# Attention with a sink and a window, then a feed-forward layer: more products of ones between TensorE's first visits

## The chip, the cores and the metric

The kernel runs on one core of a Trainium2 chip. The metric is the time of one execution in microseconds on the device, the median of several runs.

## What is computed

Queries, keys and values have 4 batches, 8 heads, 768 positions and 64 columns. Each position sees the 128 positions up to itself and the first 4 (the sink). The heads are joined to a table of 3072 rows by 512, which goes through two matrices with an ELU between them.

```python
keep = is_sink | in_window
scores = np.where(keep, scale * q @ k.T, -1e9)
a = np.exp(scores - scores.max(-1))
x = (a / (a.sum(-1) + 1e-9)) @ v
h = x @ w_in
g = np.where(h > 0.0, h, np.exp(np.minimum(h, 0.0)) - 1.0)
out = g @ w_out
```

## The kernel before, in words

The 3072 rows are cut into tiles of 128 and the tiles into ten chunks of two or three. For each chunk the attention of four pairs of heads makes the table x, and a feed-forward part runs x through the two matrices in 16 steps: the product with `w_in` (L900, writes the PSUM bank h), ELU, and the product with `w_out` (L930, adds up in acc). Attention of the next chunk is put between the steps of the feed-forward part.

The work is written as tasks, each for one engine with an estimated duration and with the tasks that it depends on (`plan.add`). `Plan.order` tries a few hundred orders with those estimates and keeps the best; `keep_order` then emits all tasks in that order and ties each engine's instructions to one another, so that every engine works through a fixed list. A task of TensorE (PE in the rows) is called a visit here. TensorE does its list strictly in that order.

The first chunk has nothing to hide behind. Its attention is `attention_f32`: for each step the scores of two heads (L599, into banks s or acc), a masked minimum on VectorE (DVE, L606), an exponential on ScalarE (ACT, L609), a transpose of the result on TensorE (L616, into one of the two banks h), a copy of that bank to the tile pt by DVE or ACT (L620), and the product with the values (L657, with L665 for the sums). The transposes write columns 0 to 255 of their bank.

TensorE also computes products that nobody reads: 128 by 128 ones times 128 by 248 ones in bf16, made by `warm`, in columns 264 to 511 of a bank. Nine stand ahead of all other work (L1278), one before the first visit (L1050). For the other visits that the plan's estimate starts before 28 us, L1052 counts how many fit between the end of the visit before and the start of this one, at 0.11 us each with 0.2 us kept free, and `filled` puts them right ahead of the visit. They go to the second bank h, or to the second bank s where the visit before starts after 7.0 us by the plan. The framework adds a semaphore wait wherever a tile that is still to be read would be written again; it follows whole tiles, here a bank.

```python
ones_k, ones_n = (nc.const_aps.tensor(1.0, [P, n], BF16) for n in (P, DM - 2 * KW))

def warm(to):
    nc.tensor.matmul(to[:, 2 * KW :], ones_k, ones_n, start=True, stop=True)
```

Of the kernel before, what the change touches and what calls it, by code (L numbers as in the profile page):

```python
# [44 lines left out]
HALF = NF // 2  # L45
PARTS = [(0, 0, HALF), (1, 0, HALF), (0, HALF, NF), (1, HALF, NF)] + [(c, 0, NF) for c in range(2, len(SIZES))]
LAG = 2
EARLY, WARM_UNTIL = 9, 28.0
NEAR = 1
WHOLE = 3  # L50
TURNED = 2
# [46 lines left out]
class Plan:  # L98
# [17 lines left out]
    def add(self, eng, dur, fn, *args, deps=(), lat=0.0, pos=None, or_=(), gap=2.0, port=None, mode=None):  # L116

        t = Task(eng, dur, fn, args, deps, lat, pos, gap, port, mode)
        for way in or_:
            t.ways[way[0]] = way[1:]  # L120
        self.tasks.append(t)
        return t
# [272 lines left out]
def fast_path(tc, ctx, first, kq, vx, wt, out, nw, inside, flag, limits):  # L395
# [9 lines left out]
    def banks(name, n):  # L405
        return rows(name, [P, 512], F32, n, psum)
# [22 lines left out]
    h_ps, s_ps, po_ps = banks("h", 2), banks("s", 2), [first["end"]]  # L429
# [572 lines left out]
    for c in range(WHOLE, len(SIZES)):  # L1002

        kts = key_tiles(CHUNKS[c])
        a = kts.index(CHUNKS[c][0])
        a = a * KW if all(any(g in ch for ch in CHUNKS[WHOLE:]) for g in kts[:a]) else 0
# [33 lines left out]
    a = add("DVE", 1.45, in_range, deps=[*seen, *exps_done[:-2], limits_])  # L1040
    a = add("DVE", 0.2, last_in_range, deps=[a, *exps_done[-2:]])
    b = add("PE", 0.1, lambda: nc.tensor.matmul(sp[:, 0:3], ones, some16, start=True, stop=True), deps=[a], pos=start - 3.0)
# [6 lines left out]
    pe = sorted((t for t in tasks if t.eng == "PE" and t.start < WARM_UNTIL), key=lambda t: t.start)  # L1049
    pe[0].fn = filled(pe[0].fn, first["warm"], h_ps[1], 1)  # L1050
    for a, b in zip(pe, pe[1:]):
        b.fn = filled(b.fn, first["warm"], s_ps[1] if a.start > 7.0 else h_ps[1], int((b.start - a.start - a.dur - 0.2) / 0.11))  # L1052
    keep_order(tc, tasks, first["spread"])


def filled(fn, warm, to, n):

    def run(*args):
        for _ in range(n):
            warm(to)  # L1060
        fn(*args)

    return run
# [5 lines left out]
def keep_order(tc, tasks, first):  # L1069

    bb = tc.nc.cur_bb.bb
    seen = len(bb.instructions)
    prev = {first.engine: first.name}
    base = tc.cur_priority
    for i, t in enumerate(tasks):
        tc.cur_priority = base + 10 * i
        t.fn(*t.args)
        new = bb.instructions[seen:]
        seen += len(new)
        for ins in new:  # L1080
            if ins.engine in prev:
                tc.add_manual_dep(ins, prev[ins.engine], mybir.DependencyInfo(mybir.DependencyClass.NoSync, mybir.DependencyReason.DATA), reason="order")
            prev[ins.engine] = ins.name
# [169 lines left out]
def attention_moe(tc, kq, vx, words_in, wt, out):  # L1253
    nc = tc.nc
    with ExitStack() as ctx:
# [51 lines left out]
        with ExitStack() as inner:  # L1307
            fast_path(tc, inner, first, kq, vx, wt, out, nw, f[:, 0:1], flag, limits)
# [38 lines left out]
```

## Time and profile before

| what | value |
|---|---|
| median of 3 runs | 616.5 us |
| lowest and highest | 615.62, 616.95 us |
| the profiled execution's own time | 616.32 us |
| its span, first to last instruction | 614.5 us |
| TensorE busy | 604.5 us, 98% |
| VectorE, ScalarE, GpSimd busy | 485.0, 450.3, 271.5 us |

The shares are means over the whole span. The change lies in its first 30 us, so the timeline of that stretch is what to read, engine by engine: start, duration, line, tiles and count, and in brackets the idle time ahead of a row with what ended it. Idle times that are shorter than 0.15 us are not shown. Rows of one kind that follow one another are merged, and a merged row of TensorE ends with the pipeline of its last product.

### The profile page before, as it was taken

How to read it: one execution, taken by the hardware profiler on the slowest of the kernel's cores; microseconds unless marked ns; L12 is line 12 of the kernel's file. 1: busy time of each engine (PE TensorE's matmuls, PEld its weight loads, DVE VectorE, ACT ScalarE, POOL GpSimd, SP SyncE). 2: the span in 40 equal slices, each digit the busy share in tenths (PEclk: the TensorE clock that was granted, in tenths of full speed). 3: DMA queues.
4: the chain of work that ended last, by engine and by line, in shares of the span. 5: the costliest groups of instructions: out<-in, count | busy, mean ns of one | idle time of the engine just before them, and what ended most of it. 6: DMA issues, size and time to landing. Idle time of an engine off the chain costs nothing.

```text
span 614.5 us, 14283 instructions
## 1 busy us (share of the span) xinstructions
PE 604.5 (98%) x4797; PEld 384.3 (63%) x4797; DVE 485.0 (79%) x1330; ACT 450.3 (73%) x1313; POOL 271.5 (44%) x545
## 2 busy tenths in 40 slices
PE   9998999999999999999999999999999999999996
PEld 6764666677665555676655556766555567665553
DVE  6998899899986657899997689999976899732232
ACT  5999999789876656888776678986766789642222
POOL 3787777345533233454333334443433435422211
PEclk9999999999999999999999999999999999999999
DMA  8688956879867256878772659898736596800001
GB/s 305 237 300 246 269 217 197 210 166 223 195 159 208 59 125 138 224 195 200 191 205 74 184 116 250 185 222 179 197 100 162 133 236 133 182 26 10 0 2 57
DMA packets 127428, 103.18 MB, mean 168 GB/s; under 512 B 96498, under 2 KB 102898, under 8 KB 127346
## 3 DMA queue, kind: packets, MB, share of 16 engines
q1 hardware_dynamic: 127200, 102.12, 64.3%
q8 instruction: 39, 0.64, 0.4%
q14 instruction: 43, 0.35, 0.2%
q10 hardware_dynamic: 146, 0.07, 0.0%
HBM read 71.75 MB, written 7.34 MB: 129 GB/s over the span
## 4 chain that ended last, share of the span: by engine, by line
PE 83%; ACT 10%; DVE 3%; issue 1%; DMA 1%; POOL 0%; DVEq 0%; ACTq 0%
PE h L900 35%; PE acc L930 29%; PE last_acc L930 6%; PE s L790 3%; PE s L791 3%; PE last_end L860 2%; PE s L860 2%; ACT w L501 2%; ACT last_acc L338 2%; ACT g L908 1%; ACT wu L341 1%; ACT gh L914 1%; ACT e L814 1%; DMA pt<-pq 1%; ACT e L609 1%
## 5 line engine op out<-in xcount | busy, mean ns | idle before, releaser
L900 PE MATMUL h<-x,w 128*128 128x256 f16 (+1 forms) x1920 | 275.7, 294 | 2.6 <-DVE gl L916 1.9
L900 PEld LDWEIGHTS <-w 128*128 128x128 f16 x1920 | 186.7, 98 | 78.2 <-issue 3.7
L919 POOL TENSOR_TENSOR gl<-g,gh 128x256 f16<-128x256 f32 (+1 forms) x143 | 119.9, 839 | 184.7 <-ACT gh L914 145.6
L930 PE MATMUL acc<-w,gh 128*128 128x512 f16 x636 | 175.0, 379 | 0.0
L930 PEld LDWEIGHTS <-gh 128*128 128x128 f16 x792 | 75.0, 98 | 66.7 <-issue 0.9
L908 ACT ACTIVATE g<-h 128x256 f32<-128x256 f32 (+1 forms) x160 | 66.8, 417 | 66.9 <-PE h L900 62.3
L914 ACT ACTIVATE gh<-g 128x256 f16<-128x256 f32 (+1 forms) x143 | 65.4, 458 | 48.7 <-DVE g L913 47.9
L930 PE MATMUL acc<-w,gl 128*128 128x512 f16 x318 | 96.9, 379 | 0.0
L814 ACT ACTIVATE e<-e,st 128x264 f32<-128x264 f32 x160 | 80.9, 506 | 17.0 <-DVE st L812 16.6
L910 DVE TENSOR_SCALAR g<-g 128x256 f32<-128x256 f32 (+1 forms) x99 | 35.5, 359 | 71.8 <-ACT g L908 70.9
L827 DVE SCALAR_TENSOR_TENSOR pq<-e,st,pq 128x256 f16<-128x256 f32 x160 | 86.0, 557 | 6.0 <-ACT pq L826 4.9
L826 ACT ACTIVATE pq<-e,st 128x256 f16<-128x256 f32 x160 | 75.1, 499 | 4.9 <-ACT g L908 2.0
L913 DVE SCALAR_TENSOR_TENSOR g<-g,h 128x256 f32<-128x256 f32 (+1 forms) x144 | 68.3, 474 | 4.8 <-ACT g L910 3.0
L812 DVE CUSTOM_DVE_ANT_0 e<-s,m 128x264 f32<-128x264 f32 x160 | 64.3, 425 | 9.2 <-PE s L791 8.3
L930 PEld LDWEIGHTS <-gl 128*128 128x128 f16 x396 | 38.1, 98 | 44.2
L716 ACT ACTIVATE kq<-kqs 128x912 f16<-128x912 f32 (+1 forms) x56 | 47.9, 860 | 6.9 <-PE s L791 5.1
L818 POOL TENSOR_SCALAR st<-st 128x2 f32<-128x2 f32 x80 | 19.3, 241 | 75.1 <-ACT e L814 66.8
L930 PE MATMUL last_acc<-w,gh 128*128 128x512 f16 (+1 forms) x126 | 45.3, 366 | 0.0
L502 POOL TENSOR_TENSOR w<-wv,w 128x512 f16<-128x512 f32 x32 | 38.0, 1192 | 9.0 <-ACT w L501 8.1
L719 DVE SCALAR_TENSOR_TENSOR kq<-kqs,kq 128x528 f16<-128x528 f32 (+1 forms) x56 | 38.1, 680 | 2.7 <-ACT kq L716 1.9
L790 PE MATMUL s<-kq 128*128 128x264 f16 x144 | 37.0, 276 | 0.6 <-ACT pq L826 0.6
L791 PE MATMUL s<-kq 128*128 128x264 f16 x144 | 36.9, 276 | 0.0
(155 smaller groups left out, 825.3 us busy)
## 6 DMA issues: line engine op xcount, KB each, us to landing
raw<-in_wt_dram SPq DMA_DIRECT2D x32, 512.0 KB, 5.7
kqs<-in_kq_dram SPq DMA_DIRECT2D x32, 456.0 KB, 3.8
kqs<-in_kq_dram SPq DMA_DIRECT2D x28, 326.0 KB, 3.5
out_dram<-wv SPq DMA_DIRECT2D x21, 256.0 KB, 4.5
vs<-in_vx_dram SPq DMA_DIRECT2D x16, 320.0 KB, 3.8
qk<-in_kq_dram SPq DMA_DIRECT2D x24, 195.0 KB, 4.5
vs<-in_vx_dram SPq DMA_DIRECT2D x16, 256.0 KB, 3.4
qk<-in_kq_dram SPq DMA_DIRECT2D x24, 163.0 KB, 4.1
```

What stands on the lines that cost most here:

```text
L790: nc.tensor.matmul(sp[:, :wd], q, hi[:, c0 : c0 + wd], start=True, stop=False)
L791: nc.tensor.matmul(sp[:, :wd], q, lo[:, c0 : c0 + wd], start=False, stop=True)
L812: red = add("DVE", 0.08 + 0.00104 * wd, lambda ee=ee, me=me, sp=sps[e], m=m, wd=wd: nc.vector.tensor_tensor_reduce(ee, sp[:, :wd], m[:, :w ...
L814: ex = add("ACT", act_us(wd, sums=True), lambda ee=ee, me=me, rs=rs[:, e : e + 1]: nc.scalar.activation(ee, ee, AF.Exp, bias=me, scale=-1. ...
L826: a = add("ACT", act_us(nb * P, True), lambda src=src, hi=hi, re=re: nc.scalar.activation(hi, src, AF.Copy, scale=re), deps=[rr])
L827: b = add("DVE", dve_us(nb * P) + 0.03, lambda src=src, hi=hi, lo=lo, re=re: nc.vector.scalar_tensor_tensor(lo, src, re, hi, ALU.mult, ALU ...
L900: nc.tensor.matmul(hp[:, :n], win[:, part, d, :], xx[:, :n], start=k == 0, stop=k == 3 * ND - 1)
L908: a = add("ACT", act_us(n) + 0.06, lambda gf=gf, hp=hp, sums=sums: nc.scalar.activation(gf, hp[:, :n], AF.Exp, scale=1.0 / G_SCALE, accum_ ...
L913: b = add("DVE", dve_us(n) - 0.035, lambda gf=gf, gd=gd, hp=hp: nc.vector.scalar_tensor_tensor(gd, gf, 0.0, hp[:, :n], ALU.min, ALU.max), ...
L914: th = add("ACT", act_us(n) - (0.03 if near else 0.0), lambda gd=gd, gh=gh: nc.scalar.activation(gh[:, :n], gd, AF.Copy), deps=[b])
L919: tl = add("POOL", pool_us(n), lambda gl=gl, gd=gd, gh=gh: nc.gpsimd.tensor_tensor(gl[:, :n], gd, gh[:, :n], ALU.subtract), deps=[th])
L930: nc.tensor.matmul(to[:, : cols.stop - cols.start], gg[:, i * P : (i + 1) * P], wout[:, part, cols], start=f == f0 and k == 0, stop=f == f ...
```

## The change

A second constant is added, and the count of products ahead of a visit changes in two ways: 0.1 us is kept free instead of 0.2, and visits that the plan starts before 8.5 us get one more.

```diff
-EARLY, WARM_UNTIL = 9, 28.0
+EARLY, WARM_BY, WARM_UNTIL = 9, 8.5, 28.0
...
     for a, b in zip(pe, pe[1:]):
-        b.fn = filled(b.fn, first["warm"], s_ps[1] if a.start > 7.0 else h_ps[1], int((b.start - a.start - a.dur - 0.2) / 0.11))
+        b.fn = filled(b.fn, first["warm"], s_ps[1] if a.start > 7.0 else h_ps[1], int((b.start - a.start - a.dur - 0.1) / 0.11 + (b.start < WARM_BY)))
```

Eleven products are added, and nothing else moves on any engine: four early (one ahead of the second scores, one between the two pairs of transposes, two ahead of the third scores) and seven later, one at each of seven visits.

TensorE's list before, from the first transposes to the third scores. `h0_184` and `h1_185` are the two banks h, `e0` to `e2` hold exponentials, `vm0_108` holds the queries and keys of the third step:

```order
L616 MATMUL h0_184<-ident_192,e0_109 128x128 [waits Activation_49,Pool_49]
L616 MATMUL h0_184<-ident_192,e0_109 128x128
L616 MATMUL h1_185<-ident_192,e1_110 128x128 [waits Activation_49]
L616 MATMUL h1_185<-ident_192,e1_110 128x128
L599 MATMUL s0_186<-vm0_108 128x132 [waits DMAHW4_49,DVE_49]
L599 MATMUL s1_187<-vm0_108 128x132 [waits DVE_49]
```

The same place with the change:

```order
L616 MATMUL h0_184<-ident_192,e0_109 128x128 [waits Activation_49,Pool_49]
L616 MATMUL h0_184<-ident_192,e0_109 128x128
L1276 LDWEIGHTS const-bfloat16-1.0
L1276 MATMUL h1_185<-const-bfloat16-1.0 128x248
L616 MATMUL h1_185<-ident_192,e1_110 128x128 [waits Activation_49]
L616 MATMUL h1_185<-ident_192,e1_110 128x128
L1276 LDWEIGHTS const-bfloat16-1.0
L1276 MATMUL h1_185<-const-bfloat16-1.0 128x248 [waits DVE_49]
L1276 LDWEIGHTS const-bfloat16-1.0
L1276 MATMUL h1_185<-const-bfloat16-1.0 128x248
L599 MATMUL s0_186<-vm0_108 128x132 [waits DMAHW4_49]
L599 MATMUL s1_187<-vm0_108 128x132
```

Three products of ones have come in, two of them behind the transposes into the same bank `h1_185`, the first of these with a wait for DVE; the scores behind them no longer carry one.

One of the later places on TensorE, around the transposes at 21.07 us and the scores at 21.44 us in the trace of before, as a difference (`s_187` is the second bank s):

```order
 L1276 MATMUL s_187<-const-bfloat16-1.0 128x248
+L1276 LDWEIGHTS const-bfloat16-1.0
+L1276 MATMUL s_187<-const-bfloat16-1.0 128x248
 L616 MATMUL last_end<-ident,e_111 128x128 x2
+L1276 LDWEIGHTS const-bfloat16-1.0
+L1276 MATMUL s_187<-const-bfloat16-1.0 128x248
 L599 MATMUL s_186<-kqs_82 128x132
 L599 MATMUL s_187<-kqs_82 128x132
```

A gap that had products has one more, and between the transposes and the scores, where there was none, one stands now.

## Rows read from the trace of the kernel before

**Rows 1.** The page: busy time by engine, and the granted clock.

```profile
PE 604.5 (98%) x4797; PEld 384.3 (63%) x4797; DVE 485.0 (79%) x1330; ACT 450.3 (73%) x1313; POOL 271.5 (44%) x545
...
PEclk9999999999999999999999999999999999999999
```

**Rows 2.** Timeline of PE, 0 to 13 us: start, us, line, tiles, count.

```profile
0.78 2.02 PE L1276 MATMUL last_acc<-const-bfloat16-1.0 128*128 128x248 bf16 x9 [0.78 <-PEq L1338]
...
5.30 0.81 PE L599 MATMUL s<-kqs 64*128 64x132 f32 x4 [0.41 <-DVE st L606]
...
6.48 1.11 PE L616 MATMUL h<-ident,e 128*128 128x128 f32 x4
7.52 0.81 PE L599 MATMUL s<-vm 64*128 64x132 f32 x4
8.27 0.69 PE L616 MATMUL h<-ident,e 128*128 128x128 f32 x2
...
11.41 0.81 PE L599 MATMUL acc<-vm 64*128 64x132 f32 x4
12.15 0.57 PE L616 MATMUL h<-ident,e 128*128 128x128 f32 x2
12.66 0.50 PE L599 MATMUL s<-vm 64*128 64x132 f32 x4
```

**Rows 3.** Line L1276, 0 to 3 and 14 to 30 us: duration ns min/median/max.

```profile
L1276 PE MATMUL last_acc<-const-bfloat16-1.0 x9: 366/411/412, 0.8 to 2.4; 128*128 128x248 bf16 x9
...
L1276 PE MATMUL s<-const-bfloat16-1.0 x32: 266/271/282, 14.8 to 29.1; 128*128 128x248 bf16 x32
```

**Rows 4.** Timeline of DVE, 7 to 9 us.

```profile
7.21 0.42 DVE L620 COPY pt<-h 128x256 f32<-128x256 f32 x1 [0.49 <-PE h L616]
...
7.63 0.42 DVE L620 COPY pt<-h 128x256 f32<-128x256 f32 x1
```

**Rows 5.** Timeline of PE, 14 to 30 us, at the products of ones.

```profile
14.81 0.81 PE L1276 MATMUL s<-const-bfloat16-1.0 128*128 128x248 bf16 x6
15.55 0.44 PE L657 MATMUL last_end<-pt,vm 128*64 128x128 f32 x4
...
19.95 1.15 PE L1276 MATMUL s<-const-bfloat16-1.0 128*128 128x248 bf16 x9
21.07 0.44 PE L616 MATMUL last_end<-ident,e 128*128 128x128 f32 x2
21.44 0.55 PE L599 MATMUL s<-kqs 64*128 64x132 f32 x4
...
28.93 0.48 PE L1276 MATMUL s<-const-bfloat16-1.0 128*128 128x248 bf16 x3 [0.26 <-DVE st L606]
29.35 0.50 PE L599 MATMUL s<-kqs 64*128 64x132 f32 x4
```

**Rows 6.** Busy time by engine in stretches: PE, PEld, DVE, ACT, POOL, clock, DMA share, GB/s.

```profile
16.00:18.00 2.00, 2.00 (x24) 1.50 (x21) 1.76 (x9) 2.00 (x8) 1.30 (x4) 1.00 0.86 304
...
22.00:24.00 2.00, 2.00 (x18) 1.57 (x18) 2.00 (x11) 2.00 (x9) 1.57 (x3) 1.00 1.04 380
```

**Rows 7.** Waits of PE from 32 to 610 us: total us, times, longest.

```profile
PE h L900 <- DVE gl L916: 1.9, 2, 1.7
PE s L790 <- ACT pq L826: 0.6, 1, 0.6
PE h L900 <- POOL w L502: 0.5, 1, 0.5
PE last_end L616 <- DVE pt L620: 0.5, 1, 0.5
```

**Rows 8.** Timeline of ACT and DVE, single rows from 6 to 29 us.

```profile
6.46 0.19 ACT L609 ACTIVATION_READ_ACCUMULATOR e<-e,st 128x1 f32 x1
...
21.16 0.28 DVE L606 CUSTOM_DVE_ANT_0 e<-s,m 128x132 f32<-128x132 f32 x1
...
28.80 0.08 DVE L606 DVE_READ_ACCUMULATOR2_ANT st<- 128x1 f32 x1
```

## The prediction, made before the change was run

> **What bounds the kernel now.** Start with the page's busy times: TensorE (PE) is busy 604.5 of 614.5 us [rows 1]. From 32 us to the end the view of waits finds little for it to wait on, 3.5 us in four groups, the longest wait 1.7 us [rows 7]; from there the span is TensorE's own work. So a change of the first 30 us moves the end by what it moves TensorE at about 30 us, nearly one for one, and the change touches nothing later.
>
> Then TensorE's timeline from 0 to 13 us [rows 2]. It sits idle 0.41 us before the second scores at 5.30; after that no idle row follows until the first feed-forward. The durations tell its clock. Nine products of ones at the start take 2.02 us, of which the last one's own 0.41 is pipeline [rows 2, 3]: (2.02 - 0.41)/8 = 0.20 us from one to the next, 248 columns at 1.2 GHz. At 19.95 nine take 1.15, with 0.27 for the last: 0.11 us, the 2.4 GHz level [rows 3, 5]. The page's granted clock says full from the start; the durations contradict it, and I go by them. The step is sharp: scores of one shape take 0.81 at 11.41 and 0.50 at 12.66 [rows 2]. So the clock rose between 12.15 and 12.66, and until then TensorE ran at half speed without a pause: there it is the bound. From 14 us on, products of ones fill TensorE's gaps [rows 5], while ScalarE (ACT) is busy 2.00 of every 2.00 us [rows 6]. There the gaps hang on ACT and VectorE (DVE).
>
> **The change part by part.** The sum is made against the profiled execution, 616.32 us (span 614.5 plus 1.82 around it); the median of the runs is 616.5, 0.18 above, and I add the sum to the median.
>
> *First product, before the scores at 5.30.* It takes 0.20 us inside an idle time of 0.41 [rows 2], so it costs nothing. If that wait ended sooner, 0.20 would show.
>
> *Second product, between the two pairs of transposes that start at 6.48.* TensorE runs them without an idle row, four by 7.59 [rows 2]. The second pair now ends 0.20 later, at 7.79.
>
> *Third and fourth product, before the scores at 7.52.* This is the step that matters. They go to the second h bank, into which the second pair of transposes has just been written; the order shows the first of the two waiting for DVE. The columns don't overlap, but the wait covers the bank. What DVE still has to do there is the copy of that bank to pt: it runs 7.63 to 8.05 now, 0.04 after the transposes end and just behind the copy of the first bank [rows 4]. With transposes ending at 7.79 it runs 7.83 to 8.25. A wait of TensorE on DVE costs another 0.05 (DVE ends at 28.88, TensorE starts at 28.93) [rows 5, 8]. Products at 8.30 and 8.50, array free at 8.70, and 0.14 for the change to scores (the last transpose, whose pipeline ends at 7.59, leaves the array at 7.59 - 0.21 = 7.38, and the scores start at 7.52): the scores start at 8.84, not 7.52. That is **1.32 us late**. Behind them in TensorE's order stands everything else: the next transposes, the value products, the next scores. DVE and ACT wait for those.
>
> *What of it reaches 13 us.* Between 7.52 and the rise no row shows TensorE idle [rows 2], so nothing absorbs the 1.32 there. If the clock rises when it did, the last 1.32 us of slow work are done behind the rise, in half the time: **0.66 us** is left.
>
> *Seven late products, 0.11 us each.* They stand before the visits at 15.55, 18.50, 21.07, 21.44, 22.52, 28.27 and 29.35. Lower bound 0: ACT has no free time there [rows 6], and what TensorE loses may be waited for anyway. Upper bound: 7 x 0.11 = 0.77, plus 0.13 at 21.44, where the lone product writes the bank that DVE reads until 21.44 (21.16 + 0.28) [rows 8] and the scores, which start at 21.44 now, come behind it: 21.44 + 0.05 + 0.11 + 0.08 for the change of kind = 21.68, 0.24 instead of 0.11. The 0.08 is 15.55 less the end of the six products before it, 14.81 + 6 x 0.11 [rows 5]. So up to 0.90. I take **0.6**, nearer the upper end: of the gaps shown, the visits at 15.55 and 29.35 follow their products within 0.1 us with no idle row, so what stands there waited for products, not for ACT.
>
> *Sum:* 0 + 0.66 + 0.6 = 1.26, say **1.3 us slower: 617.8**. Ends: 0.66 and 0.66 + 0.90 = 1.6. From 30 us on it is carried to the end [rows 7].
>
> *When the clock rises* is the unknown. Each microsecond that the rise moves is half a microsecond at the end, since slow work is worth half. In this trace it came at 12.15 to 12.66. The Trainium skill ("TensorE: Matmul & The Clock Gate", Part 1) says that the rise falls elsewhere from run to run of the same kernel, and that a model shouldn't be fitted to one such point. By the row the sum is 1.3; by that rule it is 1.3 on average, and single runs of either kernel spread by some tenths to either side. The runs shown, 615.62 to 616.95, leave room for that and don't prove it.
>
> **The rivals.** About 0.2%, 1.23 us, is what a measurement of this kernel can tell from no change: below 615.27 is faster, above 617.73 slower. My forecast lies just beyond that bound.
>
> *A. The clock rises several microseconds sooner* (faster than before). The first products fill idle or slow time; if that brings the rise to before 7.5 us, the slow stretch from 7.52 to 12.5 halves: 2.5 us saved. The wait for the copy is still there: ACT ends its fourth exponential at 6.65 [rows 8], transposes and copy follow at full clock to about 7.7, two products and the scores at 8.0, 0.5 late. With 0.6 for the late products: -2.5 + 0.5 + 0.6 = -1.4, **615.1**. A rise at 9.8 us would just cancel my 1.3, (12.4 - 9.8)/2; sooner than that it decides. For it: the 0.41 us of idle time shrinks, and the same page (section "Why this matters for your kernels") advises keeping TensorE fed to get the faster clock. Against it: TensorE has no idle row from 5.30 to the rise and ran slow all the same, and the change opens an idle time of 8.30 - 7.59 - 0.20 = 0.5 us that wasn't there. Chance 0.17.
>
> *B. The clock rises later.* The last idle time before the rise ended at 5.30; now one ends at 8.30, 3 us on. If the rise moves with it, by up to 3 us, up to 1.5 more are lost: **618.5 to 619.3**. For it: that idle time. Against it: the trace shows one rise only. Chance 0.25.
>
> *C. The late products are absorbed* by waits for ACT and only the 0.66 counts: **617.2**, within 0.2%. For it: ACT at 2.00 of 2.00 [rows 6]. Against it: ACT itself starts late, since it waits for the scores. Chance 0.13.
>
> *D. My forecast*, 0.7 to 1.6 slower, 617.2 to 618.1. Chance 0.45; it straddles the bound, about half on either side.
>
> **How the numbers follow.** Faster: A, 0.17. Within 0.2%: C and half of D, 0.13 + 0.22 = 0.35. Slower: half of D and B, 0.23 + 0.25 = 0.48. The range takes in D and C whole, A to its centre and B to near its end: 615.0 to 619.2. Slower cases alone would be 617.7 to 619.3.
>
> **What would show it.** In the timeline after: an idle row of about 0.5 us before two products on h near 8.3, put down to DVE pt, and scores near 8.8. If the scores start by 7.9, the wait isn't there and I am wrong at the main step. Scores and values at 1.2 GHz durations until about 12.5 and the shift halving there is D; 0.50 scores before 10 us is A; 0.81 scores still at 13 us is B. The first product should leave the scores at 5.30. At 29.35 the scores should start 1.1 to 1.4 later; if by 0.7, it is C. After 32 us TensorE's waits should be as before; a wait of over 0.5 us that is new there would mean that something else in the program moved.

## The result, and the profile after

The change makes the kernel slower: **619.99 us** (618.69 to 620.62, 6 runs) against 616.5 (614.8 to 616.95, 6 runs beside it), a ratio of 1.0058 [1.0042, 1.0075], 3.5 us. The sign of the forecast, 617.8, is right; its size is not, and 619.99 lies outside the range of 615.0 to 619.2. The profiled execution took 620.38 us, 4.06 more than the one before. How much later TensorE stands at each place tells where that comes from:

| place on TensorE | before, us | after, us | later by |
|---|---|---|---|
| second scores | 5.30 | 5.94 | 0.64 |
| third scores | 7.52 | 9.46 | 1.94 |
| scores into acc, clock at full in both | 14.11 | 15.66 | 1.55 |
| values behind the first late products | 15.55 | 17.22 | 1.67 |
| scores, second late group | 21.44 | 23.57 | 2.13 |
| first L900 | 22.77 | 24.77 | 2.00 |
| transposes of 26.95 | 26.95 | 30.50 | 3.55 |
| first L930 | 32.12 | 35.91 | 3.79 |
| start of the last product | 609.68 | 613.87 | 4.19 |

Two steps make it: one before 10 us, and one of 1.5 us between 25 and 31 us, of which the prediction knew nothing.

The timeline of TensorE after, 4 to 15 us, which answers to [rows 2] (start, duration, line, tiles, count, and in brackets the idle time ahead with what ended it):

```profile
4.95 0.39 PE L1276 MATMUL h<-const-bfloat16-1.0 128*128 128x248 bf16 x1
5.94 0.81 PE L599 MATMUL s<-kqs 64*128 64x132 f32 x4 [0.60 <-DMA kqs<-in_kq_dram]
...
7.60 0.41 PE L1276 MATMUL h<-const-bfloat16-1.0 128*128 128x248 bf16 x1
7.81 0.64 PE L616 MATMUL h<-ident,e 128*128 128x128 f32 x2
8.96 0.57 PE L1276 MATMUL h<-const-bfloat16-1.0 128*128 128x248 bf16 x2 [0.52 <-DVE pt L620]
9.46 0.81 PE L599 MATMUL s<-vm 64*128 64x132 f32 x4
...
13.35 0.57 PE L599 MATMUL acc<-vm 64*128 64x132 f32 x4
...
14.21 0.50 PE L599 MATMUL s<-vm 64*128 64x132 f32 x4
```

And the timeline of DVE beside it, which answers to [rows 4]:

```profile
7.85 0.42 DVE L620 COPY pt<-h 128x256 f32<-128x256 f32 x1 [0.50 <-PE h L616]
...
8.48 0.42 DVE L620 COPY pt<-h 128x256 f32<-128x256 f32 x1
```

The second scores wait for a load. It landed at 5.17 in the profile of before (where the row names DVE, which ended beside it, at 5.16) and at 5.80 here, so the scores start 0.64 us later. That is chance: over all the profiles it lands 5.2 to 5.8 us after the start, whatever the kernel, and the scores follow 0.10 to 0.19 behind. The rest of the 1.94, **1.30 us**, is the forecast wait: DVE's copy of the second bank h ends at 8.90, the two products start at 8.96 behind an idle time of 0.52, the scores at 9.46. The scores then step from 0.81 to 0.57 and 0.50 us at 13.35 to 14.21, where before they did so at 12.66 [rows 2]: the clock rose about 1.1 us later.

The second step stands in the timeline of all engines. First before the change, 22 to 27 us:

```profile
21.92 0.61 PE L1276 MATMUL s<-const-bfloat16-1.0 128*128 128x248 bf16 x4
22.57 0.28 DVE L606 CUSTOM_DVE_ANT_0 e<-s,m 128x132 f32<-128x132 f32 x1
22.79 0.45 DVE L342 TENSOR_SCALAR wu<-raw 128x512 uint16<-128x512 uint16 x1
23.12 1.16 POOL L502 TENSOR_TENSOR w<-wv,w 128x512 f16<-128x512 f32 x1 [0.32 <-ACT w L501]
24.21 0.46 DVE L343 TENSOR_SCALAR wu<-raw 128x512 uint16<-128x512 uint16 x1
24.56 0.45 DVE L342 TENSOR_SCALAR wu<-raw 128x512 uint16<-128x512 uint16 x1
...
26.35 0.41 DVE L679 TENSOR_TENSOR rx<-last_end,rx 128x256 f32<-128x256 f32 x1
26.95 0.38 PE L616 MATMUL last_end<-ident,e 128*128 128x128 f32 x2
```

Then the same work with the change, 24 to 31 us:

```profile
24.00 0.71 PE L1276 MATMUL s<-const-bfloat16-1.0 128*128 128x248 bf16 x5
...
24.71 1.16 POOL L502 TENSOR_TENSOR w<-wv,w 128x512 f16<-128x512 f32 x1 [0.33 <-PE s L1276]
24.75 0.30 DVE L606 CUSTOM_DVE_ANT_0 e<-s,m 128x132 f32<-128x132 f32 x1 [0.23 <-PE s L1276]
24.97 1.22 DVE L342 TENSOR_SCALAR wu<-raw 128x512 uint16<-128x512 uint16 x1
26.57 1.16 POOL L502 TENSOR_TENSOR w<-wv,w 128x512 f16<-128x512 f32 x1 [0.33 <-DVE st L622]
27.07 0.97 DVE L343 TENSOR_SCALAR wu<-raw 128x512 uint16<-128x512 uint16 x1
27.81 0.85 POOL L340 TENSOR_SCALAR wu<-raw 128x512 uint16<-128x512 uint16 x1
27.94 1.04 DVE L342 TENSOR_SCALAR wu<-raw 128x512 uint16<-128x512 uint16 x1
30.03 0.41 DVE L679 TENSOR_TENSOR rx<-last_end,rx 128x256 f32<-128x256 f32 x1
30.50 0.44 PE L616 MATMUL last_end<-ident,e 128*128 128x128 f32 x2 [1.01 <-DVE rx L679]
```

L342 and L343 unpack a weight on DVE, L502 subtracts for another weight on GpSimd (POOL); neither waits for the other. Before, DVE's first L342 began 0.33 us ahead of GpSimd's L502 and took 0.45. Now it begins 0.26 behind and takes 1.22; the next two begin behind a GpSimd instruction as well and take 0.97 and 1.04 instead of 0.46 and 0.45. That is 0.77 + 0.51 + 0.59 = 1.87 us on DVE, and TensorE idles 1.01 for DVE's L679 at 30.50.

Why DVE fell behind stands two rows above. The masked minimum (L606) at 24.75 reads the second bank s, and the five unread products of 24.00 to 24.71 are written into that bank behind the scores. It starts 0.04 us after the products end, as at 22.57 before; but before, DVE was busy until then, and now it idles 0.23. All told DVE comes to L342 2.18 us later than before, GpSimd to L502 only 1.59 later: DVE has lost 0.59 against GpSimd, 0.32 of it between the two minima here (24.24 and 24.75, where before they stood at 22.38 and 22.57) and the rest at the visits before.

The waits of TensorE from 32 to 614 us answer to [rows 7] (total us, times, longest):

```profile
PE h L900 <- DVE gl L916: 1.9, 2, 1.7
PE s L790 <- ACT pq L826: 1.0, 1, 1.0
PE h L900 <- POOL w L502: 0.6, 1, 0.6
PE last_end L616 <- DVE pt L620: 0.5, 1, 0.5
PE s L1276 <- DVE st L606: 0.3, 1, 0.3
```

They are nearly those of before; the one that grew, 0.6 to 1.0, is the step from 3.79 to 4.19 in the table.

### The profile page after: what moved, and what is told of

The parts are those of the page before. It is cut to its first block, busy times and chain, and to the rows that moved or that the text cites. A ratio compares the mean times of both kernels' runs of the same rounds, so it can differ in the third digit from the quotient of the medians.

```text
span 618.5 us, 14302 instructions
## 1 busy us (share of the span) xinstructions
PE 606.1 (98%) x4808; PEld 385.4 (62%) x4808; DVE 487.0 (79%) x1330; ACT 450.6 (73%) x1313; POOL 271.7 (44%) x545
## 4 chain that ended last, share of the span: by engine, by line
PE 84%; ACT 9%; DVE 4%; DMA 1%; issue 1%; SPq 0%; ACTq 0%; DVEq 0%
PE h L900 35%; PE acc L930 29%; PE last_acc L930 6%; PE s L790 3%; PE s L791 3%; PE last_end L860 2%; PE s L860 2%; ACT w L501 1%; ACT last_acc L338 1%; ACT g L908 1%; ACT gh L914 1%; ACT e L814 1%; DMA pt<-pq 1%; ACT wu L341 1%; DMA kqs<-in_kq_dram 1%
## 5 line engine op out<-in xcount | busy, mean ns | idle before, releaser
L900 PE MATMUL h<-x,w 128*128 128x256 f16 (+1 forms) x1920 | 275.6, 294 | 2.6 <-DVE gl L916 1.9
L900 PEld LDWEIGHTS <-w 128*128 128x128 f16 x1920 | 186.8, 98 | 78.1 <-issue 3.7
L930 PE MATMUL acc<-w,gh 128*128 128x512 f16 x636 | 175.0, 379 | 0.0
L930 PEld LDWEIGHTS <-gh 128*128 128x128 f16 x792 | 75.1, 98 | 66.7 <-issue 0.9
L930 PE MATMUL acc<-w,gl 128*128 128x512 f16 x318 | 96.9, 379 | 0.0
L930 PEld LDWEIGHTS <-gl 128*128 128x128 f16 x396 | 38.2, 98 | 44.2
L930 PE MATMUL last_acc<-w,gh 128*128 128x512 f16 (+1 forms) x126 | 45.3, 366 | 0.0
L502 POOL TENSOR_TENSOR w<-wv,w 128x512 f16<-128x512 f32 x32 | 38.0, 1193 | 9.5 <-ACT w L501 8.1
L790 PE MATMUL s<-kq 128*128 128x264 f16 x144 | 36.9, 276 | 1.0 <-ACT pq L826 1.0
```

Of the source, the lines that this page charges most:

```text
L790: nc.tensor.matmul(sp[:, :wd], q, hi[:, c0 : c0 + wd], start=True, stop=False)
L900: nc.tensor.matmul(hp[:, :n], win[:, part, d, :], xx[:, :n], start=k == 0, stop=k == 3 * ND - 1)
L930: nc.tensor.matmul(to[:, : cols.stop - cols.start], gg[:, i * P : (i + 1) * P], wout[:, part, cols], start=f == f0 and k == 0, stop=f == f ...
```

## Experiments

Three theories are told apart. **Theory 1**: two parts, the wait at the bank h with the later rise of the clock, and DVE's lost turns at GpSimd, which come from the late products in the bank s. **Rival 2**: the early part is all. **Rival 3**: late products cost only their own 0.11 us each. All diffs are against the line of the change (L1052); `A` stands for its count and `B` for the count of before. Times are medians, this kernel's first and then that of the kernel before in the same series. Ratios carry 95% intervals; they compare all the runs and needn't be the quotient of the two medians.

### One part alone

```diff
+        n = A if b.start < WARM_BY else B    # e1, h2: early products only
+        n = B if b.start < WARM_BY else A    # e2: late products only
```

> Only the four early products of the change; the later gaps are filled as before. Theory 1 (the wait on the bank h and the clock make one part of the loss, VectorE's lost turns at GpSimd near 25 us the other, and these come from the late products): the scores before 9.5 us start 1.3 late as in the changed kernel, half of it is left at 15 us, with the clock's rise up to 1 us later 0.5 more; VectorE and GpSimd are late by the same amount there, so L342 takes 0.45 us at each of its places. 0.7 to 1.3 slower than before, 617.2 to 617.8. Rival 2 (everything comes from the early wait and the clock, late products cost nothing): as slow as the changed kernel, 3.5 slower, 620. Rival 3 (late products cost only their own 0.11 us each): 0.8 less than the changed kernel, 619.2.

> Only the seven late products; nothing is added before 8.5 us of the plan. Theory 1: VectorE's minimum of the second head's scores waits for the products that follow them into the same bank, VectorE comes 0.5 to 0.7 us behind GpSimd near 25 us, and L342 and L343 take about 1 us instead of 0.45 at three places: 1.5 to 2.5 slower than before, 618.0 to 619.0. Rival 2 (the early part is all): no slower than 0.2 us, 616.5. Rival 3 (0.11 us each): 617.1 to 617.3, L342 at 0.45.

> The four early products alone a second time, to narrow the interval of the early part. Theory 1: the scores after the second transposes 1.3 late, half of it left, and the clock's rise later than in the kernel before in most runs: 0.7 to 1.3 slower than before, L930 9.3 us after the first L900. Rival: same as before, all of the change's loss is VectorE's lost turns.

Early alone: 617.2 against 615.93, 1.0015 [0.9995, 1.0035]; again: 617.57 against 616.03, 1.0039 [1.0015, 1.0062], so **1.3 and 1.5 us** by the medians (0.9 and 2.4 by the ratios). Late alone: 618.16 against 615.93, 1.0027 [1.0008, 1.0047], **2.2 us** (1.7 by the ratio). Together 3.5 to 3.8 by the medians, as the change. From the first L900 to the first L930 the profiles take 9.34 us (e1) and 11.15 (e2), against 9.35 before and 11.14 with the change: the second step comes with the late products alone. Rival 2 falls. The early part is less sure in size: the interval of the first series holds 1, and 1.5 lies above the 0.7 to 1.3 expected. e2 has no early products, yet its L342 starts behind L502 and is long all the same:

```profile
23.32 1.16 POOL L502 TENSOR_TENSOR w<-wv,w 128x512 f16<-128x512 f32 x1 [0.32 <-PE s L1277]
23.56 1.23 DVE L342 TENSOR_SCALAR wu<-raw 128x512 uint16<-128x512 uint16 x1
```

### The same products in banks that nobody waits for

```diff
+        to = s_ps[1] if a.start > 7.0 else first["acc"]                    # e3: early ones elsewhere
+        to = acc[1] if a.start > 13.0 else s_ps[1] if a.start > 7.0 else h_ps[1]         # e4: late ones
+        to = acc[1] if a.start > 13.0 else s_ps[1] if a.start > 7.0 else first["acc"]    # f1: both
```

> The changed kernel, with its early products written to last_acc, which nobody reads until 13 us, so that no copy has to be waited for. Theory 1: no idle row before the third scores, which start 0.6 later than before instead of 1.9 with the same landings; 0.3 of that and no late rise are left at 15 us: 0.7 to 1.2 faster than the changed kernel, 618.8 to 619.3, with L342 still near 1 us. Rival 2: back to before, 616.5 to 617. If products early in the program bring the clock up sooner, scores take 0.50 before 12 us and it is faster than 618.

> The changed kernel, with the products after 15 us written to acc1, which nobody reads between 15 and 31 us. VectorE's minimum no longer waits for a product. Theory 1: VectorE reads the second scores as soon as they are there, L342 takes 0.45 or comes far enough ahead, and the 1.8 us near 25 us are gone: 1.5 to 2.5 faster than the changed kernel, 617.5 to 618.5. Rival 2: same as the changed kernel, 620. Rival 3: same as the changed kernel, since every product is still there.

> The changed kernel with all its products, the early ones written to last_acc and those after 15 us to acc1, so that nobody waits for a bank that they share. Theory 1 (the loss comes from waits that the products' banks bring, not from the products): none of the three is left; no idle row before the third scores, L342 at 0.45 us, 0.2 of TensorE's early time is lost and VectorE reads the second head's scores up to 0.5 sooner: 0.7 slower to 0.7 faster than before, 615.2 to 616.6 against 615.9. Rival (the products' own time counts, 11 of them): 0.8 slower or more, 616.7 and up. If the early products bring the clock up sooner in most runs: 1 us or more faster than before, under 614.9.

e3: 618.19 against 615.93, 1.0032 [1.0015, 1.0048], about what the late products cost alone, though 0.6 below the 618.8 that was expected at least. e4: 617.53 against 615.93, 1.0017 [1.0000, 1.0034], about what the early ones cost alone. f1 has **every product of the change**, only in other banks: 616.67 against 616.48, 0.9997 [0.9984, 1.0010]. So the loss isn't in the products' own time but in who waits for the banks that they write. For the early ones this is a net figure, since the clock rose at 10.82 in f1's profile and at 12.47 before, and no run parts the two. For the late ones TensorE's rows settle it: from the scores of 14.11 to the first L900 its delay against before grows by 0.44 us in e2 and 0.45 in the change, but by 0.11 in e4 and 0.10 in f1, where nobody waits. In e3's timeline of TensorE the wait at the bank h is gone, and the scores come with no idle row:

```profile
4.79 0.39 PE L1276 MATMUL last_acc<-const-bfloat16-1.0 128*128 128x248 bf16 x1
5.30 0.81 PE L599 MATMUL s<-kqs 64*128 64x132 f32 x4
...
7.60 0.62 PE L1276 MATMUL last_acc<-const-bfloat16-1.0 128*128 128x248 bf16 x2
8.15 0.77 PE L599 MATMUL s<-vm 64*128 64x132 f32 x4
...
10.61 0.50 PE L599 MATMUL acc<-vm 64*128 64x132 f32 x4
```

Here the load came early, and the second scores start at 5.30 as before although a product stands ahead of them. In e4's timeline, DVE's minimum no longer waits for the five products, and L342 is ahead of L502 again:

```profile
23.23 0.71 PE L1276 MATMUL acc<-const-bfloat16-1.0 128*128 128x248 bf16 x5
23.49 0.27 DVE L606 CUSTOM_DVE_ANT_0 e<-s,m 128x132 f32<-128x132 f32 x1
23.68 0.28 DVE L606 CUSTOM_DVE_ANT_0 e<-s,m 128x132 f32<-128x132 f32 x1
23.90 0.45 DVE L342 TENSOR_SCALAR wu<-raw 128x512 uint16<-128x512 uint16 x1
24.27 1.16 POOL L502 TENSOR_TENSOR w<-wv,w 128x512 f16<-128x512 f32 x1 [0.33 <-ACT w L501]
```

L900 to L930 takes 8.96 us there, less than the 9.35 of before: there, too, the products in the second bank s held DVE a little.

### Late products without the rest of the change

```diff
+        n = B + 5 * (19.0 < a.start < 19.5)    # f4: five more at one visit; g1: two
```

> The kernel before with five more products at one place alone, behind the scores at 21.44 us. Theory 1: VectorE's minimum at 22.57 us waits for them, about 0.5 us, L342 starts at 23.3 instead of 22.8, behind GpSimd's L502 (23.12), and takes about 1.2 us; L343 and the second L342 lose their turns too: 1.5 to 2.2 slower than before. Rival (products cost their own time): 5 x 0.11 = 0.55 slower, L342 at 0.45.

> The kernel before with two more products, instead of five, behind the scores at 21.44 us. Theory 1 (VectorE loses its turn only if L342 comes after GpSimd's L502 has started, 0.33 us behind it in the kernel before): L342 starts at about 23.0, still ahead of 23.1, and takes 0.45 us: 0 to 0.4 slower than before. Rival (each product that stands there costs in proportion, five cost 2.1): 0.8 to 0.9 slower.

Five products at one visit of the kernel before, 0.55 us of TensorE by 0.11 each [rows 3, 5], cost 2.1: 618.62 against 616.48, 1.0041 [1.0025, 1.0056]. L342 starts 0.22 us behind L502, takes 1.25 us, and L900 to L930 takes 11.06. Two products cost nothing that can be measured, 615.91 against 615.97, 0.9995 [0.9976, 1.0014]; there L342 still comes first, by 0.11 us. The timelines of f4 and then of g1:

```profile
23.42 1.16 POOL L502 TENSOR_TENSOR w<-wv,w 128x512 f16<-128x512 f32 x1 [0.32 <-PE s L1276]
23.64 1.25 DVE L342 TENSOR_SCALAR wu<-raw 128x512 uint16<-128x512 uint16 x1
```

```profile
22.72 0.46 DVE L342 TENSOR_SCALAR wu<-raw 128x512 uint16<-128x512 uint16 x1
22.83 1.33 POOL L502 TENSOR_TENSOR w<-wv,w 128x512 f16<-128x512 f32 x1 [0.33 <-ACT w L501]
```

It is a step, not a slope, within what g1's interval allows (it ends at 0.9 us): a delay that left the order alone cost nothing that shows, one that turned it cost about 1.8 us. Rival 3 falls.

### The change with the turn forced back

```diff
+    nc.gpsimd.tensor_copy(spot[0:1, :], u.bitcast(F32)[0:1, 0:1])    # h1: one element of what L342 writes, read ahead of that L502
```

> The changed kernel with all eleven products, in their banks; the one L502 that starts near 24.7 us is made to wait for the L342 that it overtook, by a copy of one number of what L342 writes. Theory 1 (VectorE's L342 is long because GpSimd's L502 runs): that L342 takes 0.45 instead of 1.22 us; L502 is 0.9 late and may still meet L343, so 0.8 to 1.6 of the 1.8 us come back: L930 9.6 to 10.4 us after the first L900 instead of 11.1, and 0.8 to 1.6 faster than the changed kernel, 618.1 to 618.9 against a kernel before of 616.0. Rival (L342 is long for another cause, the products or a transfer): L342 near 1.2 still, 11.1 us, as slow as the changed kernel.

> The changed kernel again, beside the same runs of the kernel before. Theory 1: L342 near 1.2 us, L930 11.1 us after the first L900, 2.5 to 4 slower than before. If the loss of the first comparison was the chip's: less than 2 slower.

The change was measured once more (g4): 619.74 against 615.97, 1.0056 [1.0036, 1.0076]. With GpSimd made to let L342 go first: 618.07 against 616.03, 1.0045 [1.0032, 1.0059]; the median is **1.7 and 1.9 us below** the two of the change, though GpSimd now idles. The ratios put less between them, 0.0011 and 0.0013 or some 0.7 us, and their intervals overlap, so the conclusion rests on the rows as well. The timeline of h1 (its L503 is L502 of the others):

```profile
25.34 0.46 DVE L342 TENSOR_SCALAR wu<-raw 128x512 uint16<-128x512 uint16 x1
25.94 0.18 POOL L1064 COPY spot<-wu 1x1 f32<-1x1 f32 x1 [1.19 <-DVE wu L342]
26.09 1.15 POOL L503 TENSOR_TENSOR w<-wv,w 128x512 f16<-128x512 f32 x1
26.67 0.90 DVE L343 TENSOR_SCALAR wu<-raw 128x512 uint16<-128x512 uint16 x1
27.46 0.44 DVE L342 TENSOR_SCALAR wu<-raw 128x512 uint16<-128x512 uint16 x1
```

The first and the third DVE instruction take 0.46 and 0.44 us; the second, which still starts behind GpSimd, takes 0.90. The stretch from the first feed-forward product to the first one with `w_out` takes 9.98 us instead of 11.14, 1.16 less with two collisions of three gone. All eleven products are there, in their banks; only the order of two engines was changed, by a copy of one number that takes GpSimd 0.18 us. So the long DVE instructions are shown to come from that order. What stays of the loss, 2.0 us by the medians, is the early part and the collision left.

### Is there something to win?

```diff
+        n, to = B, (acc[1] if a.start > 13.0 else s_ps[1] if a.start > 7.0 else h_ps[1])    # f2, g3, i2
+        n, to = (A if b.start < WARM_BY else B), (s_ps[1] if a.start > 7.0 else first["acc"])    # f3
+        n, to = ((A if a.start < 5.0 else 0) if b.start < WARM_BY else B), (the banks of f1)    # g2
+        n, to = (A if b.start < WARM_BY else B), (the banks of f1)    # i1
```

> The kernel before with as many products as it has; those after 15 us go to acc1 instead of the second bank s. Theory 1: VectorE's minimum of the second head's scores need not wait for the products behind them (at 18.66, 21.16 and 22.57 us it stands behind 7, 9 and 4 of them), VectorE comes up to 0.3 us sooner and L342 keeps its 0.45 us: 0 to 0.6 faster than before. Rival: same, since ScalarE's chain is what ends last there.

> The four early products alone, written to last_acc; later gaps filled as before. Theory 1: no wait; 0.6 of slow time at most before the third scores, half of it left: 0 to 0.4 slower than before if the clock rises when it did, and up to 1.5 faster in runs where it rises near 9 us. In the first experiment of this kind the clock rose at 8.8 us. Rival (the early products cost in whatever bank): 0.7 to 1.3 slower, as with the wait.

> The late products in number as before, to acc1; of the early ones only the first, in the idle time before the second scores, to last_acc. Theory 1: nothing waits for it and VectorE's minimum waits for no product; L930 starts about 8.9 us after the first L900 instead of 9.35: 0.3 to 0.8 faster than before. Rival: same, the gain at 31 us is lost again further on.

> The kernel before with its products after 15 us in acc1, a second time, to narrow the interval. Theory 1: 0.3 to 0.6 faster than before. Rival: same.

> The version that the runs so far point to: the four early products in the bank acc, which nobody waits for there, and the late products in the second bank acc with the counts of before. Theory 1: the early products bring the clock's rise from about 12.3 to about 9 to 11 us, worth 0.7 to 1.5 us, and cost 0.6 us by their own time at the lower clock; the late ones elsewhere save the 0.4 us that they saved in the earlier profiles. Sum 0.5 to 1.3 us less than the kernel before: a ratio of 0.998 to 0.999. Rival 3 (only their own time counts): the early products cost 0.6 us and give nothing back, ratio 1.001.

> The kernel before with its late products in the second bank acc, for the third time: 0.9991 and 0.9988 so far, each with an interval that holds 1. Theory 1: 0.4 us between the first feed-forward products are saved, ratio 0.999. Rival 3: 1.000.

| kernel | median, us | before, us | ratio |
|---|---|---|---|
| f2 | 615.91 | 616.48 | 0.9991 [0.9977, 1.0004] |
| g3, the same | 615.72 | 615.97 | 0.9988 [0.9970, 1.0006] |
| i2, the same | 615.73 | 615.73 | 1.0001 [0.9991, 1.0012] |
| f3 | 616.47 | 616.48 | 1.0004 [0.9989, 1.0019] |
| g2 | 615.51 | 615.97 | 0.9997 [0.9977, 1.0016] |
| i1 | 615.98 | 615.73 | 1.0007 [0.9998, 1.0017] |

No version is shown to beat the kernel before. The hope for i1 fell: in its profile the clock rose earlier (scores of 0.50 us at 11.76), but the interval of its ratio shuts out the 0.998 to 0.999 of Theory 1 and holds the 1.001 of Rival 3. That the products' 0.20 us apiece at the lower clock eat what the rise brings is the likely reading; no run shows it by itself. The 0.4 us that f2 and g3 save between L900 and L930 is too small to be shown: the third series has 1.0001.

## Why the prediction was wrong

**The wait at bank h: right.** Forecast 1.32 us between the scores and where they stood, measured 1.30 beside the later load; the idle row forecast as about 0.5, DVE pt, reads 0.52. e3 and f1 take the bank away, and the wait and its cost go with it.

**First and second product: right.** In e3 the second scores start at 5.30 with the first product ahead of them, as before; and with the change the second pair of transposes starts 0.21 us behind its product (7.60 and 7.81), the 0.20 that was charged.

**What of it reaches 13 us: mis-sized, 0.66 forecast, 1.3 to 1.5 measured (e1, h2).** The forecast held the rise of the clock where it was. By the traces' records of the granted clock, which begin at its rise (12.47 before, 13.53 with the change), it came at 12.75 to 14.67 us, median 13.7, in the six profiles with that wait (after, e1, e4, g4, h1, h2) and at 10.95 to 16.95, median 12.2, in the eight without it and without products at the third scores (before, e2, f2, f4, g1, g2, g3, i2). With a rise later by 1.5 the shift behind it is (1.32 + 1.5)/2 = 1.4. The same sum holds in each of the six: half of what the third scores and the rise are late by, against before, gives what the scores of 14.11 are late by, to about 0.1 us (1.50 and 1.55 in the change, 1.40 and 1.40 in h2, 1.99 and 1.93 in h1). The later rise is rival B, at half of the 3 us that it allowed. The medians of the two groups scatter too much for more than the direction, and why the rise came later stays open.

**Seven late products, 0.6 (0 to 0.90): the step that failed.** They cost 2.2 us (e2, 1.7 by its ratio). The prediction charged TensorE for them and asked whether ACT's waits hide that; it didn't ask who else waits for the bank s that they are written into, and so put DVE's wait at nothing. DVE's minimum does wait. I had used the very same rule, that a wait covers a whole bank, two paragraphs earlier for the bank h, and for the lone product at 21.44, but not for the groups written behind scores that DVE is still to read. What was charged hardly came: up to the first L900, behind five of the seven visits, it is 0.1 us where nobody waits (e4, f1), near rival C's nothing. What was left out came instead: 0.3 us more up to there from the waits at bank s (0.44 in e2), and then the turn, since the 0.6 us that DVE lost against GpSimd put their order round. The turn cost 1.6 to 1.9 (the stretch from L900 to L930 in e2 against e1 and in f4 against g1, the medians of h1 against the change).

**Sum.** 1.3 to 1.5 and 2.2 instead of 0.66 and 0.6: 3.5 to 3.7 us, and 3.5 was measured. The upper end, 619.2, was rival B's; no rival had the late products cost more than themselves.

**After 32 us: right.** What TensorE has lost by then it loses to the end, plus 0.4 at the wait of L790, in the one pair of profiles. The new wait of over 0.5 us that I named as a sign of something else stands at 30.50, just ahead of the window that I had set for it.

## What to carry to other kernels

A product that nobody reads is still a write: list who is to read anything else in the tile it goes to, on every engine, because where waits follow whole tiles each of them now waits for it; put it in a tile without readers, as f1 did. And where two engines use the same resource in turns that no wait fixes, look at how many tenths of a microsecond keep them in order: here a delay smaller than that cost nothing that shows, and a larger one was paid at the price of the lost turn.

## What the runs showed of the hardware

**DVE behind GpSimd.** A DVE tensor_scalar from 128x512 uint16 to 128x512 uint16 takes 0.45 us alone and 0.90 to 1.25 when it starts well within a GpSimd instruction. (The L343 of 24.21 before the change begins only 0.07 us before L502 ends, and takes 0.46.) In the change and in h1 each of the four ended 0.31 to 0.33 us after that GpSimd instruction, however long ago it had started: 24.97 + 1.22 = 26.19 against 24.71 + 1.16 = 25.87, then 28.04 against 27.73, 28.98 against 28.66, and in h1 27.57 against 27.24. GpSimd's own instructions grew less behind DVE: L502 took 1.21 instead of 1.16 at 28.75 in the change and 1.33 in g1, L340 0.85 at 27.81 instead of 0.78. The Trainium skill ("SBUF — State Buffer", section "SBUF: two separate sides") says that VectorE and GpSimd share a pair of ports under an exclusive lock, and that whichever starts first holds it for its whole instruction. The trace agrees in that the late one ends at a fixed time behind the early one, though that time is 0.31 to 0.33 us and not the whole 0.45 that it takes alone; no run here shows in which mode L342 works, on which that rule depends.

**The clock's rise moves from run to run.** The eighteen profiles have it between 8.76 and 16.95 us. One kernel alone had 11.92, 12.20 and 16.95 (f2, g3, i2); in the last, scores still take 0.81 us at 13.06. Its last product starts 2.0 us later than in the other two, 611.79 against 609.76 and 609.73, so a microsecond of rise costs about 0.4 at the end. In the four kernels with all the early products and no wait (e3, f1, f3, i1) it came at 8.76 to 11.01, but at 10.95 also in g1, which has none of them. What sets it was not tried further.

```profile
11.70 0.81 PE L599 MATMUL acc<-vm 64*128 64x132 f32 x4
...
13.06 0.81 PE L599 MATMUL s<-vm 64*128 64x132 f32 x4
```

**The end scatters, too.** The two profiles of the early products alone, 618.42 and 616.15 us, stand within 0.08 us of one another at the first L930 (33.29 and 33.37), 1.0 apart at the last product (611.15 and 610.15), and another 1.2 apart in what lies behind it. The end of a single profile of this kernel can't carry a term of a microsecond. Medians of the same kernel from different series agree within 0.4 us: 617.2 and 617.57, 619.99 and 619.74, 615.91, 615.72 and 615.73.
